# The row swap of two filter blocks moved from TensorE matmuls to GpSimd copies, and the order of the jobs set anew

## The chip, the cores and the metric

The kernel runs on one core of one Trainium2 chip. The metric is the device time of one execution in microseconds (us). The engines are named as in the profile: PE is TensorE's matmul, PEld its weight load, DVE is VectorE, ACT is ScalarE, POOL is GpSimd, SP is SyncE. A q behind a name (POOLq, SPq) is the engine's queue, which issues DMAs.

## The reference

Two independent branches, each 2048 tokens by 576 columns, and their results side by side. Everything is bfloat16.

```python
def _A_ref(x, wqkv, wo):            # H = 32 heads of 18; window W = 8, dilation 2
    q, k, v = ...                   # x @ wqkv, split by head
    idx = pos[:, None] - off[None, :]          # 8 earlier tokens, two apart
    logits = einsum(q, k[idx]) * scale         # -1e9 where idx < 0
    o = einsum(softmax(logits), v[idx])
    return o @ wo

def _B_ref(q, k, v, shift_k, ssm_k, ssm_D):
    k_shift = sum of 4 taps of k, weighted by shift_k
    kv = k_shift * v
    y = irfft(rfft(kv, 2S) * rfft(ssm_k, 2S))[:S]     # causal convolution per column
    y = y + kv * ssm_D
    return q * y

return concatenate([a, b], axis=-1)
```

## The kernel before, in words

Everything stays on chip. Branch A projects q, k and v transposed, multiplies q by shifted k on DVE (jobs `L`), sums over a head's 18 rows with matmuls (`G`), takes the softmax (`sm`), multiplies by v on DVE (`V`), sums over the window with identity matmuls (`A`) and projects (`O`). Branch B cuts the sequence into four blocks of 512 tokens. Each block of kv (`T` on DVE, then `M` on PE) and each block m of the filter `ssm_k` (`F`) is folded into even and odd parts, taken to the spectrum with sine tables (`x` for kv, `K` for the filter), multiplied block by block on DVE (`p`), summed on PE (`z`), and brought back (`i`, `b`, `g`).

The filter block m arrives by a transposing DMA in `kTok(m)`: partition = token within a chunk of 128, four chunks of 576 columns. `fold_filter(m)` (job `Fm`, L591 to L609) makes from chunks 0 to 3 the reversed sums with matmuls against 128x128 constants. A reversal by `flip1`/`flip2r` maps row p to row 128 - p, so that row 0 is left over: it has to come from row 0 of the other chunk. For blocks 0 and 1 the rows 0 of the chunks 0 and 1 are first swapped in memory, by six small DMAs of SP through a `spare` row (`first_rows`, job `Fr`, L577 to L581). For blocks 2 and 3 nothing is swapped: the reversal `flip0` leaves row 0 empty and an extra pair of matmuls against `corner` or `corner2`, which are zero but for one element, fills it in. `negate(m)` (job `Nm`, L589, on DVE) keeps a scaled copy of the old row 0. Behind the fold come two copies from PSUM on ACT (L604) and three accumulating DMAs that POOL issues (L606 to L609). The filter units `Kmcg` (L566, L567, copied out by ACT at L617) with c = 1 need the fold alone, those with c = 0 also the DMAs.

The order of the work is written by hand in the table `ORDER`: a list of job names. The program is recorded in that order, and each engine and each queue gets its instructions in it, one behind the other; an instruction waits for semaphores and holds up what stands behind it on its own engine. PSUM is four slots handed round in the order of the jobs. Other names in this document: `Lom` is a copy of a filter chunk by a DMA that POOL issues (L649), `SV` gives out the memory of v, `Z2` clears its pads on POOL (L366, L368), `RGn` regroups the weights of v on ACT (L779), `Un` are later accumulating DMAs of POOL (L625), `I` and `X5` are small preparations on PE.

## Time and profile before

| | |
|---|---|
| three runs | 207.15, 207.64, 208.27 us; median 207.64 |
| the profiled execution | 207.14 us, of which the span of the trace is 205.4 |
| PE busy | 197.5 us, 96% of the span |
| DVE busy | 187.9 us, 91% |
| ACT busy | 155.6 us, 76% |
| POOL busy | 64.0 us, 31% |
| DMA | 38.48 MB moved, mean 187 GB/s |

The share of busy time is an average over stages. PE and DVE are both nearly full; which of them ends a wait differs from stage to stage. In the rows below the first number of a timeline is the start in us from the span's start, the second the time; "x2" behind the shapes means two instructions merged into one row, with the time from the first start to the last end.

### The profile page before, as it was taken

Reading aid. Unit: us, or ns where it says so; the run is one execution under the profiler, and the core shown is the slowest. Engines: PE = TensorE matmul, PEld = TensorE weight load, DVE = VectorE, ACT = ScalarE, POOL = GpSimd, SP = SyncE. Lnnn points to the kernel's source line nnn. Section 1 sums busy time; section 2 is a strip of 40 time slices with the busy share of each in tenths; the row PEclk is TensorE's granted clock in tenths of the full one; section 3 lists DMA queues with packets and bytes.
Section 4 is the critical chain, followed back from the end, with each engine's and each line's share of the span. In section 5 each row is a group of like instructions: output and inputs, shape, how many; then the busy total and the mean of one; then the engine's idle time right before and its main releaser. Section 6 shows DMA issues by size and latency. Waiting matters only on the chain.

```text
span 205.4 us, 5096 instructions
## 1 busy us (share of the span) xinstructions
PE 197.5 (96%) x2112; PEld 111.2 (54%) x2122; DVE 187.9 (91%) x143; ACT 155.6 (76%) x223; POOL 64.0 (31%) x106
## 2 busy tenths in 40 slices
PE   7999999999999999999999999999999999999990
PEld 2534344434664656534354566766667767676560
DVE  7579999999999999999999999999999994599961
ACT  3798894858999999957776688876778877655660
POOL 8999910022266492300560000022090002030210
PEclk9999999999999999999999999999999999999997
DMA  6999999999239669999799990969899204853645
GB/s 201 304 321 250 213 317 351 187 220 297 84 48 125 91 91 193 176 200 219 153 246 203 245 224 14 177 229 264 163 246 246 91 3 165 180 153 122 173 158 150
DMA packets 34916, 38.48 MB, mean 187 GB/s; under 512 B 17523, under 2 KB 28911, under 8 KB 34894
## 3 DMA queue, kind: packets, MB, share of 16 engines
q1 hardware_dynamic: 26668, 24.29, 45.9%
q0 software_dynamic: 5760, 11.36, 29.3%
q10 hardware_dynamic: 2466, 2.51, 3.6%
q8 instruction: 16, 0.26, 0.5%
q14 instruction: 6, 0.05, 0.1%
HBM read 13.11 MB, written 4.72 MB: 87 GB/s over the span
## 4 chain that ended last, share of the span: by engine, by line
PE 67%; DVE 18%; DMA 7%; issue 4%; ACT 2%; SPq 1%; DVEq 0%
PE ps_z L968 10%; DVE tB L516 9%; PE ps_wo L887 8%; PE ps_inv L1003 7%; PE ps_acc L823 7%; PE ps_fx L681 7%; PE ps_proj L321 7%; DVE xw L519 7%; PE ps_fk L566 5%; PE ps_log L719 4%; DMA xw<-in_A_wqkv_dram 3%; DMA kj<-in_B_k_dram 2%; PE ps_fk L567 2%; DMA Ks<-in_B_ssm_D_dram 2%; PE ps_wo L879 2%
## 5 line engine op out<-in xcount | busy, mean ns | idle before, releaser
L321 PE MATMUL ps_proj<-xw 128*128 128x512 bf16 x151 | 37.3, 380 | 0.9 <-issue 0.6
L705 DVE TENSOR_TENSOR av<-qk 128x4096 bf16<-128x4096 bf16 (+1 forms) x16 | 31.7, 2013 | 0.1
L321 PEld LDWEIGHTS <-xw 128*128 128x128 bf16 x160 | 14.0, 98 | 18.2 <-issue 4.5
L981 ACT ACTIVATE av<-ps_z 128x768 bf16<-128x768 f32 x23 | 17.3, 810 | 6.5 <-PE ps_z L968 5.9
L617 ACT ACTIVATE Ks<-ps_fk 128x576 bf16<-128x576 f32 x32 | 19.4, 750 | 0.4 <-PE ps_fk L567 0.4
L516 DVE TENSOR_TENSOR tB<-kj,skb 128x4608 bf16<-128x4608 bf16 (+1 forms) x8 | 19.3, 2417 | 0.1
L354 ACT ACTIVATE qk<-ps_proj 128x1024 bf16<-128x1024 f32 x14 | 14.2, 1024 | 6.6 <-PE ps_proj L321 4.8
L683 ACT ACTIVATE xw<-ps_fx 128x576 bf16<-128x576 f32 x32 | 18.5, 666 | 0.7 <-PE ps_fx L681 0.7
L625 POOL DMA_DIRECT2D Ks<-Ks x8 | 11.0, 1654 | 26.0 <-PE ps_wo L879 18.6
L949 DVE TENSOR_TENSOR qk<-xw,Ks 128x2304 bf16<-128x2304 bf16 x14 | 18.6, 1353 | 0.0
L887 PE MATMUL ps_wo<-qk 128*128 128x288 bf16 x128 | 17.9, 287 | 0.0
L681 PE MATMUL ps_fx<-xw,TB 128*128 128x288 bf16 x128 | 17.5, 286 | 0.0
L566 PE MATMUL ps_fk<-Ks,TB 128*128 128x384 bf16 x62 | 16.3, 326 | 0.2
L1003 PE MATMUL ps_inv<-av,TI 128*128 128x288 bf16 (+1 forms) x112 | 15.9, 292 | 0.0
L823 PE MATMUL ps_acc<-av,ident 64*64 64x512 bf16 x160 | 15.3, 378 | 0.0
L567 PE MATMUL ps_fk<-Ks,TB 128*128 128x192 bf16 x62 | 15.2, 246 | 0.0
L681 PEld LDWEIGHTS <-TB 128*128 128x128 bf16 x128 | 12.0, 98 | 5.5 <-issue 2.1
L949 DVE TENSOR_TENSOR v<-xw,Ks 128x2304 bf16<-128x2304 bf16 x7 | 9.5, 1354 | 5.6 <-PE ps_z L968 5.6
L887 PEld LDWEIGHTS <-qk 128*128 128x128 bf16 x128 | 11.9, 98 | 4.8 <-issue 2.1
L812 DVE TENSOR_TENSOR av<-Ks,v 128x4096 bf16<-128x4096 bf16 x6 | 13.6, 2286 | 0.1
L354 ACT ACTIVATE v<-ps_proj 128x1024 bf16<-128x1024 f32 x9 | 9.3, 1035 | 5.8 <-PE ps_proj L332 3.0
L826 ACT ACTIVATE qk<-ps_acc 128x1024 bf16<-128x1024 f32 x8 | 8.2, 1023 | 7.1 <-PE ps_acc L823 7.1
(194 smaller groups left out, 447.1 us busy)
## 6 DMA issues: line engine op xcount, KB each, us to landing
Ks<-Ks POOLq DMA_DIRECT2D x8, 576.0 KB, 8.1
TB<-av SPq DMA_DIRECT2D x12, 256.0 KB, 5.3
kj<-in_B_k_dram SPq DMA_DIRECT2D x6, 504.0 KB, 7.0
vt<-in_B_v_dram SPq DMA_DIRECT2D x8, 288.0 KB, 5.1
Ks<-av SPq DMA_DIRECT2D x8, 256.0 KB, 5.8
out_dram<-qk ACTq DMA_DIRECT2D x5, 288.0 KB, 5.1
Ks<-in_A_x_dram SPq DMA_DIRECT2D x2, 576.0 KB, 5.1
xw<-in_A_wqkv_dram SPq DMA_DIRECT2D x2, 576.0 KB, 5.8
```

The lines of the kernel that those rows point to most:

```text
L321: nc.tensor.matmul(ps[:, jp, :], wq(kb, comp, 128 * ct, 128), xT(kb, 1024 * jj + 512 * jp, 512), **se)
L354: nc.scalar.activation(view(t, o + pad + 1024 * jj, [[512, 2], [1, 512]]), ps[:], ACT.Copy)
L516: tt(to, view(kj, row * D, [[D, n], [D, 4], [1, D]]), view(skb, row * D, [[D, n], [0, 4], [1, D]]), ALU.mult)
L566: nc.tensor.matmul(o[:, 0:2], w, rhs[:, 0:2], start=start, stop=stop)
L617: nc.scalar.activation(view(Ks, k_at(m, cs ^ (m & 1)) + 96 * gi, [[768, 3], [384, 2], [1, 96]]), acc3(ps), ACT.Copy, scale=(PSG, MSG)[cs][ ...
L681: nc.tensor.matmul(ps[:, pm, 0:HD], TX[:, 2 * pm + c, 128 * gi:128 * gi + 128], kv[:, 2 * c + pm, HD * h:HD * h + HD], start=(c == 0), sto ...
L705: tt(view(P, at, [[step, 4], [256, nj], [1, 256]]), view(t, o + 256 * hh, [[0, 4], [512, nj], [1, 256]]), view(tk, ok + 2 + 8 * ug + 256 * ...
L823: nc.tensor.matmul(acc[64 * o:64 * o + 64, h, :], ident[64 * h:64 * h + 64, 64 * h:64 * h + 64], view(P[s], 256 * u, [[2048, 2], [1, 256]] ...
L887: nc.tensor.matmul(ps[:, r, 0:HD], oT(hh, j + 2 * r, t)[:, o:o + 128], wo[:, t // 2, t % 2, HD * h:HD * h + HD], start=(t == 0 and not fli ...
L949: tt(product_home(n), view(xw, HB * XG[i] + QTR * t, [[HB, 3], [1, QTR]]), view(Ks, k_at(j - i, 0) + QTR * t, [[HB, 3], [1, QTR]]), ALU.mult)
L968: nc.tensor.matmul(view(ps, 512 * h, [[192, 2], [96, 2], [1, 96]])[o:o + 64], w[64 * h:64 * h + 64, 64 * h:64 * h + 64], pr[64 * h:64 * h ...
L1003: nc.tensor.matmul(ps[:, c, 0:n], TI[:, sl, pm, 128 * c:128 * c + 128], Yall(j % 2, pm, sl, slice(c0, c0 + n)), start=(pm == 0 and sl == 0 ...
```

## The change

Blocks 2 and 3 are now swapped too, by three copies each on POOL: old row 0 of chunk 0 to the spare row, row 0 of chunk 1 to chunk 0, spare to chunk 1 (`swap_rows`, jobs `RS3` and `RS2`). The fold then has the same form for all blocks: 8 matmuls and not 12. The constants `flip0`, `corner` and `corner2` go, and so do the POOL instructions that made them (a copy, two clears of 128x128 and two of one element); `pad` keeps their memory. `negate` of the blocks 2 and 3 reads the spare row and so comes behind the first copy. The table `ORDER` is written anew from its first line to its last.

```diff
-    flip0 = main.tile([128, 128], BF16, name="flip0")
-    corner = main.tile([128, 128], BF16, name="corner")
-    corner2 = main.tile([128, 128], BF16, name="corner2")
+    pad = main.tile([128, 384], BF16, name="pad")
...
-    nc.gpsimd.tensor_copy(flip0[:], flip1[:])
...
-    nc.gpsimd.memset(corner[:], 0.0)
-    nc.gpsimd.memset(corner2[:], 0.0)
-    nc.gpsimd.memset(corner2[0:1, 0:1], 2.0 ** 0.5)
-    nc.gpsimd.memset(corner[0:1, 0:1], 1.0)
...
-    spare = [view(Ks, k_at(1, 0) + D * m, [[1, D]])[0:1] for m in range(2)]
+    spare = [view(Ks, k_at(1, m // 2) + D * (m - m // 2), [[1, D]])[0:1] for m in range(NBL)]
+
+    def swap_rows(m):
+        for to, of in ((spare[m], row(m, 0)), (row(m, 0), row(m, 1)), (row(m, 1), spare[m])):
+            nc.gpsimd.tensor_copy(to, of)
...
     def negate(m):
-        nc.vector.tensor_scalar(minus_of(m), spare[m] if m < 2 else row(m, 0), -0.5 * ROOT, None, ALU.mult)
+        nc.vector.tensor_scalar(minus_of(m), spare[m], -0.5 * ROOT, None, ALU.mult)
...
     def fold_filter(m):
-        kt, swapped = kTok(m), m < 2
+        kt = kTok(m)
...
-            turns = [((flip2r, flip1)[c] if swapped else flip0, 1 - c), ((identn0, identn)[c], 2 + c)]
-            if not swapped:
-                turns.insert(1, ((corner2, corner)[c], c))
+            turns = [((flip2r, flip1)[c], 1 - c), ((identn0, identn)[c], 2 + c)]
...
         job(f"N{m}", negate, m)
+        if m > 1:
+            job(f"RS{m}", swap_rows, m)
```

Of the table, the lines around the two folds:

```diff
-    M00 k03b k12a M21 Lo0 q13b N1 k12b x020 x021 Z2 x001 RG2 k24a k24b L000 L002 x010 RG0 F3 F2 K312 L001 K311
-    K211 K212 RG1 K210 K310 RG3 G000 G001 L003 F1 N0 L004 G002 L010 G003 K300 G004 L012 K303 K313 K302 K201 K202
...
+    k12b k10a' N2 k10b q10b L000 M00 Z2 k24a' k24b L002 M21 k13a' k13b x020 x021 x001 x010 RG0 L001 RG1 RG2 F3
+    F2 G000 L003 K311 K313 K213 K312 K211 K310 G001 RG3 L004 G002 L010 K212 N1 F1 G003 L011 G004 L012 K302 K303
```

On POOL the place is the end of the filter's arrival. Before, behind the preparations (L501, L503), stand the copies Lo3, Lo2, Lo1 (L649), the accumulation of `ssm_D` (L578), Lo0, and then the clears of v's pads, the copy of a pad of q or k (L357) and the first DMA of the fold (L606):

```order
L501 MEMSET TB 1x512
L503 MEMSET TB 1x128 x4
L649 DMA Ks<-Ks 128x576 x3
L578 DMA Ks<-in_B_ssm_D_dram 1x16x36
L649 DMA xw<-Ks 128x576
L366 MEMSET v 128x4x16
L368 MEMSET v 64x16
L357 DMA qk<-qk 64x16
```

Now, with line numbers three to seven lower:

```order
L646 DMA Ks<-Ks 128x576 x3
L575 DMA Ks<-in_B_ssm_D_dram 1x16x36
L646 DMA xw<-Ks 128x576
L572 COPY Ks<-Ks 1x576 x6
L359 MEMSET v 128x4x16
L361 MEMSET v 64x16
L350 DMA qk<-qk 64x16
```

The six copies stand between Lo0 and the clears, and all of POOL's later work stands behind them.

On DVE the place is the change from the taps of the last kv block (the last of them L535) to the first products of branch A (L705). Before:

```order
L516 TENSOR_TENSOR tB<-kj,skb 128x4608
L519 TENSOR_TENSOR xw<-xw,tB 128x2304 x2
L535 TENSOR_TENSOR xw<-xw,vt 128x2304
L589 TENSOR_SCALAR Ks<-Ks 1x576 x3
L705 TENSOR_TENSOR av<-qk 128x4096
L705 TENSOR_TENSOR v<-qk 128x4x1024
```

Now:

```order
L509 TENSOR_TENSOR tB<-kj,skb 128x4608
L512 TENSOR_TENSOR xw<-xw,tB 128x2304 x2
L528 TENSOR_TENSOR xw<-xw,vt 128x2304
L586 TENSOR_SCALAR Ks<-Ks 1x576 x2
L702 TENSOR_TENSOR av<-qk 128x4096
L702 TENSOR_TENSOR v<-qk 128x4x1024
```

The first two negations, N3 and N2, stay ahead of the first product; N1 has moved behind it. Both wait for POOL now, N3 for the first copy and N2 for the fourth.

On ACT, around the copies of the folds F3 and F2 (L604, now L599), before:

```order
L683 ACTIVATE xw<-ps_fx 128x2x3x96 x3
L779 ACTIVATE xw<-Ks 128x576
L354 ACTIVATE qk<-ps_proj 128x1024
L683 ACTIVATE xw<-ps_fx 128x2x3x96
L779 ACTIVATE xw<-Ks 128x576
L604 ACTIVATE Ks<-ps_rev 128x576 x4
L617 ACTIVATE Ks<-ps_fk 128x6x96 x4
```

Now:

```order
L347 ACTIVATE qk<-ps_proj 128x1024
L680 ACTIVATE xw<-ps_fx 128x2x3x96 x4
L776 ACTIVATE xw<-Ks 128x576 x3
L599 ACTIVATE Ks<-ps_rev 128x576 x4
L612 ACTIVATE Ks<-ps_fk 128x6x96 x6
```

Three regroupings of v's weights, and not two, stand ahead of the folds' copies.

More of the change, by code (lines that the diff above doesn't have):

```diff
@@ L20 @@
 ORDER = """
-    I0 k02a I1 k00a k00b T0 T1 k01a' Lk2 S1 k02b k01b X5 q24a Lv2 T2 M01 Lk3 q24b Lv3 T3 Ex Lf3 q10a' q11a' N3
-    q11b q10b Lo3 k13a q12a' q12b k13b M10 Lf2 N2 Lo2 k10a Lf1 Lo1 k10b Lf0 M11 q13a' Lw Fr SV k11a' k11b k03a
-    M00 k03b k12a M21 Lo0 q13b N1 k12b x020 x021 Z2 x001 RG2 k24a k24b L000 L002 x010 RG0 F3 F2 K312 L001 K311
-    K211 K212 RG1 K210 K310 RG3 G000 G001 L003 F1 N0 L004 G002 L010 G003 K300 G004 L012 K303 K313 K302 K201 K202
-    K213 L011 F0 K203 G010 K200 K301 L013 U3 K103 G011 L014 G012 L100 RG4 K101 K100 G013 G014 K102 K111 K112
@@ L26 @@
-    K010 K110 K013 K113 U2 sm0a sm0b K012 K001 v24a v24b L101 G100 G101 sm0c K000 K011 L102 L103 v02a K002 K003
-    sm0d D0 G102 G103 v02b L104 G104 L110 L111 v00a' M20 v00b ak02 M30 D1 ak01 ak00 G110 L112 G111 L113 v01a'
-    v01b v11a v11b G112 L114 D2 M31 G113 V04 x030 G114 sm1a V11 v10a' v10b V10 x011 A04 v13a' sm1b v13b v03a
-    sm1c sm1d V12 v03b A10 v12a' x221 v12b x220 V13 V20 x330 A11 V21 x200 x211 x321 x031 V22 x300 A20 x301 x310
-    x000 x311 x331 Wl V23 x201 A21 D3 V34 A34 ax00 O000' D4 x231 x210 x230 x100 x131 x111 V40 V41 A40 O100' x101
@@ L31 @@
-    x110 x320 O001 V42 V43 A41 x130 U1 ak10 D5 V50 x120 Tx2 V51 x121 O010 p000 V52 A50 ax01 z000 O110 V53 ax02
-    p010 ax10 Tk2 O011' O101 A51 z010 O020' O021 p020 z020 Q0 p101 O111' i000 p200 i02880 p100 z100 z101 Q1 i001
-    i02881 p110 p111 z110 z111 p120 p121 z120 z121 p201 Tx3 z200 p202 z201 z202 i100 p210 z210 p211 b0288 p212
-    z211 z212 O120' i101 O121 b00 b10 O030' O031 i12880 p220 p221 z220 z221 p222 z222 Tk3 i200 p301 g0 p302
-    i12881 i201 O130 b1288 p300 z300 z301 z302 p303 z303 i22880 Q2 O131 p310 z310 p312 p311 p313 z311 z312 z313
@@ L36 @@
-    g1 Q3 i22881 i300 p320 p321 z320 p322 b2288 p323 i301 b20 g2 z321 z322 z323 b30 i3384L g30 g3384
+    T0 T1 k00a' k00b k02a Lk2 Lv2 Lk3 k02b S1 Ex k01a' k01b k03a Lv3 Lf3 k03b X5 k11a k11b q11a' Lo3 q11b Lf2
+    Lo2 Lf1 Lo1 M01 q24a Lf0 I1 q24b M10 Lw q12a' q12b T2 Fr I0 Lo0 q13a q13b k12a q10a T3 SV RS3 N3 RS2 M11
+    k12b k10a' N2 k10b q10b L000 M00 Z2 k24a' k24b L002 M21 k13a' k13b x020 x021 x001 x010 RG0 L001 RG1 RG2 F3
+    F2 G000 L003 K311 K313 K213 K312 K211 K310 G001 RG3 L004 G002 L010 K212 N1 F1 G003 L011 G004 L012 K302 K303
@@ new lines @@
+    K301 K200 K210 K203 N0 F0 K202 G010 K300 L013 K201 U3 RG4 G011 L014 G012 K103 K112 G013 K101 G014 K110 K102
+    L100 K113 K011 K100 K013 K111 sm0a sm0b K001 U2 v24a v24b G100 L101 G101 L102 sm0c sm0d K010 K000 K012 G102
+    L103 L104 K002 K003 D0 v02a v02b G103 L110 v00a G104 L111 x000 v00b G110 L112 ak02 v01a' v01b G111 L113
+    v11a' v11b G112 L114 M30 G113 x030 G114 D1 M20 v10a' v10b V04 v03a sm1a sm1b V10 v13a v13b A04 sm1c V11 D2
+    sm1d D3 V12 v03b A10 V13 D4 M31 v12a' v12b x321 x320 A11 x310 x011 V20 x201 x331 V21 x210 A20 V22 x200 V23
@@ new lines @@
+    V34 x330 x220 x301 x031 x211 A21 ax01 Wl A34 V41 O000' V40 U1 V42 x231 x221 D5 x230 Tx2 x130 x120 x311 A40
+    V43 x100 ax00 x121 x101 ak00 x300 O001 A41 O100' V50 x110 x131 x111 V51 A50 O010' O110 ak10 p000 V53 Tk2 V52
+    Q0 ak01 p010 z000 ax02 ax10 O011' O101 A51 p020 z010 p110 p101 O020' O021 z020 p100 Q1 O111' i000 i02880
+    p111 z100 p120 z101 p121 i001 p200 i02881 z110 p201 z111 z120 z121 z200 z201 Tx3 b0288 p202 z202 O120' p210
+    i100 p211 p212 z210 p222 z211 z212 Tk3 O030' p221 i101 O121 b00 p220 b10 O031' z220 p301 z221 z222 p303 g0
@@ L37 @@
+    Q2 i12880 i200 i12881 i201 p300 O130 z300 p302 z301 b1288 z302 z303 b20 i22880 O131 p310 p311 z310 p312 p313
+    g1 z311 z312 p322 z313 p320 p321 i22881 i300 z320 p323 b2288 i301 g2 z321 z322 z323 b30 i3384L Q3 g30 g3384
 """
```

## The prediction

> **What bounds the kernel now.** I read the page first: busy time and the chain that ended last.

> ```profile
> PE 197.5 (96%) x2112; PEld 111.2 (54%) x2122; DVE 187.9 (91%) x143; ACT 155.6 (76%) x223; POOL 64.0 (31%) x106
> ...
> PE 67%; DVE 18%; DMA 7%; issue 4%; ACT 2%; SPq 1%; DVEq 0%
> ```

> PE is full, two thirds of the chain are its own work, so a matmul less is worth its time, and a wait of PE is lost for good. The DVE share of the chain lies ahead of 50 us. Then I took the stage of the folds by windows of 5 us; each pair is busy time and count, PEclk the granted clock.

> ```profile
> core 0: us, PE busy (x) PEld busy (x) DVE busy (x) ACT busy (x) POOL busy (x), PEclk, DMA share, GB/s
> 50.00:55.00 5.00, 5.00 (x42) 2.80 (x42) 4.90 (x8) 4.95 (x7) 1.64 (x4) 1.00 0.53 172
> 55.00:60.00 5.00, 4.87 (x40) 3.55 (x39) 5.00 (x4) 5.00 (x9) 2.13 (x4) 1.00 0.02 3
> 60.00:65.00 5.00, 4.74 (x53) 2.31 (x52) 4.89 (x4) 5.00 (x8) 4.49 (x5) 1.00 1.02 143
> ```

> PE, DVE and ACT are all full here, POOL is not. Third, PE's own timeline through the folds F3 and F2 (54.67 to 57.63), the first filter unit, the first two head sums (61.06) and F1 (62.22):

> ```profile
> 54.67 0.41 PE L601 MATMUL ps_rev<-Ks,flip 128*128 128x288 bf16 x2
> 54.92 0.41 PE L601 MATMUL ps_rev<-Ks,corner 128*128 128x288 bf16 x2
> 55.16 0.41 PE L601 MATMUL ps_rev<-Ks,identn 128*128 128x288 bf16 x2
> ...
> 57.63 0.32 PE L566 MATMUL ps_fk<-Ks,TB 128*128 128x384 bf16 x1
> ...
> 58.42 0.32 PE L566 MATMUL ps_fk<-Ks,TB 128*128 128x384 bf16 x1
> ...
> 61.06 1.22 PE L719 MATMUL ps_log<-av,E 128*32 128x512 bf16 x16
> 62.22 0.42 PE L601 MATMUL ps_rev<-Ks,flip2r 128*128 128x288 bf16 x2
> ```

> Fourth, what POOL and DVE do when POOL has to read SBUF. The next two fences are timelines: the preparations early on, and the place where the copies are put in.

> ```profile
> 15.65 2.56 DVE L516 TENSOR_TENSOR tB<-kj,skb 128x4608 bf16<-128x4608 bf16 x1
> 15.82 2.53 POOL L287 COPY flip<-flip 128x128 bf16<-128x128 bf16 x1
> 18.24 2.75 DVE L519 TENSOR_TENSOR xw<-xw,tB 128x2304 bf16<-128x2304 bf16 x2
> 18.30 1.44 POOL L288 COPY flip2r<-flip 128x128 bf16<-128x128 bf16 x1
> 19.88 0.19 POOL L291 MEMSET corner<- 128x128 bf16 x1
> 21.02 1.36 DVE L535 TENSOR_TENSOR xw<-xw,vt 128x2304 bf16<-128x2304 bf16 x1
> 21.26 1.51 POOL L297 TENSOR_SCALAR ident<-ident 128x128 bf16<-128x128 bf16 x1
> 22.30 2.64 DVE L516 TENSOR_TENSOR tB<-kj,skb 128x4608 bf16<-128x4608 bf16 x1
> 22.74 2.59 POOL L298 TENSOR_SCALAR identn<-ident 128x128 bf16<-128x128 bf16 x1
> 25.40 0.51 POOL L501 MEMSET TB<- 1x512 bf16 x1
> ```

> ```profile
> 50.22 2.75 DVE L519 TENSOR_TENSOR xw<-xw,tB 128x2304 bf16<-128x2304 bf16 x2
> 50.44 0.86 POOL L578 DMA_DIRECT2D Ks<-in_B_ssm_D_dram  x1 [2.13 <-DVE tB L516]
> 51.00 0.88 POOL L649 DMA_DIRECT2D xw<-Ks  x1
> 53.01 1.36 DVE L535 TENSOR_TENSOR xw<-xw,vt 128x2304 bf16<-128x2304 bf16 x1
> 54.28 0.73 DVE L589 TENSOR_SCALAR Ks<-Ks 1x576 bf16<-1x576 bf16 x3
> 54.94 2.27 DVE L705 TENSOR_TENSOR av<-qk 128x4096 bf16<-128x4096 bf16 x1
> 57.14 2.27 DVE L705 TENSOR_TENSOR v<-qk 128x4096 bf16<-128x4096 bf16 x1
> ```

> A POOL copy that starts beside a DVE TENSOR_TENSOR lasts until that instruction's end and a little: L287 ends at 18.35, the DVE instruction at 18.21; L288 at 19.74, its neighbour (the first of two, 1.36 each) at 19.60. L297 and L298 do the same with 22.77 behind 22.38 and 25.33 behind 24.94. The MEMSET at 19.88, which reads nothing, takes 0.19 in the midst of a DVE instruction. So a POOL instruction with an input gets one chance per DVE instruction, at its end.

> [...]

> **The change part by part.**

> *Eight matmuls less.* Three pairs start 0.245 apart (54.67, 54.92, 55.16), 0.1225 a matmul: 8 x 0.1225 = 0.98 us off PE, in a stage where PE is full. The preparations that go (2.53, 0.19 and smaller) lie on POOL's early stretch, where nobody waits: nothing.

> *The price of a copy of 1x576.* No row shows one. From MEMSET: 128 columns take 0.19, 512 take 0.51, so 0.83 ns a column. The COPY of 128 columns lasts 0.14 beyond the DVE end, so one of 576 some 0.14 + 448 x 0.00083 = 0.51; I take 0.5 behind a DVE instruction and 0.6 alone. Low end 0.14, as the small copy; high end 1.75, if it went by L297's overhang of 0.39 x 4.5. I keep to the COPY, it is the same operation. DVE loses 0.08 to L297's 128 columns, so 0.08 x 4.5 = 0.36 to a copy (0 to 0.5).

> *When the swaps are done.* POOL is free of Lo0's issue at 51.00 + 0.88 = 51.88; what stands ahead of it in its queue, and SP's loads, are in the same order as before. DVE's second L519 runs until 52.97: copy 1 ends at 53.5. L535 is held to 53.36 and ends at 54.73; copy 2 ends at 55.2. N3 (0.25) goes in between or beside; copy 3 ends at 55.9, and with it RS3. Copy 4 ends at 56.5, N2 runs until 56.9, copy 5 slips in until 57.1, and the first product starts at 57.2 in place of 54.94. It runs 2.27, to 59.5: copy 6 starts beside it and ends at 60.0. So F3 can start at 56.0, F2 at 60.1.

> *PE at the folds.* The same jobs of PE stand ahead of F3 in both tables, so PE is there at 54.67 again: it waits 56.0 - 54.67 = 1.3 us. F3 takes 0.98, to 57.0; F2 waits 60.1 - 57.0 = 3.1. PE takes its queue in order, and the filter units that need F3 alone stand behind F2: nothing fills the wait.

> *What comes back.* ACT does all of RG0 to RG2 in the waits, ahead of the folds' copies, and so is ahead later, where PE waited for it: the unit at 57.63 took 0.79 and not 0.49, F1 until 63.72 and not 63.20.

> ```profile
> 63.72 0.61 PE L719 MATMUL ps_log<-v,E 128*32 128x512 bf16 x8
> ```

> That is 0.3 + 0.5 = 0.8 us to win back (0 to 0.8; I take all, since ACT gains more than that).

> *The granted clock.* Windows around the last matmuls:

> ```profile
> 1.30:4.72 3.42, 3.42 (x10) 1.27 (x10) 3.00 (x9) 1.87 (x3) 3.35 (x8) 1.00 0.80 255
> ...
> 195.86:199.28 3.42, 3.15 (x65) 2.31 (x54) 2.65 (x4) 1.85 (x4) 0.60 (x1) 1.00 0.25 83
> 199.28:202.69 3.41, 1.25 (x22) 0.74 (x19) 1.93 (x4) 0.68 (x2) 0.00 (x0) 1.00 0.93 263
> 202.69:205.40 2.71, 0.00 (x0) 0.00 (x0) 0.00 (x0) 0.00 (x0) 0.00 (x0) 0.50 0.23 57
> ```

> After a stretch of 3.41 us with 1.25 of PE work the clock is at 0.50. Between 54.67 and 60.1 PE would have 0.98 of work in 5.4 us. A stretch of 3.41 at half clock costs PE 1.7 of work; part of it lies in the wait itself: 0 to 1.7, I take 0.85.

> [...]

> *Work behind the copies.* POOL's clears of v's pads and F3's DMAs come at about 60.5 instead of 58.42 (the first POOL DMA of the fold). The units that need them stand behind F1 and four more head sums and are late by the same wait: nothing more, up to 0.5 if the cover is short. DVE is 2.3 behind at the first product and 0.36 more at copy 6; PE is behind by more, so DVE is not the bound.

> ```profile
> 58.42 1.28 POOL L606 DMA_DIRECT2D Ks<-Ks  x1 [2.26 <-ACT Ks L604]
> ```

> *The rest of the table.* The same work on each engine, elsewhere in the order. Ahead of the folds PE is full both ways; behind, single waits of some 0.3 us come and go: nothing, within 0.7 either way.

> The sum: -0.98 + 1.3 + 3.1 - 0.8 + 0.85 = +3.5 us on the profiled execution's 207.14: 210.6. The median before, 207.64, is 0.5 above that execution, so 210.6 is +1.4% by it.

> **The rivals.** (1) *In time, faster.* If a copy takes its low end of 0.14, copy 3 ends at 54.9 and F3 waits 0.3; copy 4 ends near 55.1, and copies 5 and 6 both begin before the first product does, some 0.25 us later: F2 doesn't wait. -0.98 + 0.3 = -0.7: 206.4. It is decided there: below 0.25 a copy, copy 6 is ahead of the product. For it: 0.14 is what the trace shows of a COPY. Against: that one has 128 columns, and MEMSET shows a price per column. (2) *No change.* The same short copies, but copy 6 falls beside the first product, from 55.4 to 57.7: F2 starts at 57.9, where PE came at 56.0: -0.98 + 0.3 + 1.9 - 0.8 = +0.4: 207.5. (3) *The clock stays*: the waits are 1.3 and 3.1, each shorter than the 3.41 of the rows' stretches, so every such stretch holds some work, if little: 3.5 - 0.85 = 2.65: 209.8. For it: only one stretch of the trace is so empty, and it is the last. [...] (4) *Copy 5 too is caught by the first product*: one more DVE instruction of 2.27 until F2: 212.9. What decides is whether POOL or DVE is first behind copy 4.

> **How the numbers follow.** Forecast 0.40, the clock stays 0.20, copy 5 caught 0.12, no change 0.14, in time 0.14. A measurement of this kernel tells about 0.5%, 1.0 us, from no change. Slower by more: 0.40 + 0.20 + 0.12 = 0.72; within: 0.14; faster by more: 0.14. The late cases alone span 209 to 213. Reaching to the case of no change and leaving out the one in time, the range is 206.9 to 213.0.

> **What the profile after would show.** Six COPY rows on POOL of 1x576, most ending just behind a DVE end; L000 near 57; a gap or a stretched wait of PE for POOL ahead of both folds, the second above 2 us; F2 near 60; the granted clock below 1.00 in a window behind. If the copies take 0.2 us each, or stand between DVE instructions without waiting, or F2 starts before 57.5, the forecast is wrong.

## The result, and the profile after

The changed kernel takes 217.01 us (median of 4 runs, 216.45 to 217.25), the kernel before 207.47 on the same chip (207.15 to 208.27): a ratio of 1.0436 with a 95% interval of 1.0412 to 1.0460. The direction was forecast. The size was not: 9.5 us, where 3.5 were forecast on the profiled execution and 3.0 on the median, and the time lies outside the range. The profiled execution of the changed kernel has a span of 215.1 us (before 205.4).

The page: busy time, the granted clock in 40 slices of 5.4 us, and the chain that ended last.

```profile
PE 199.4 (93%) x2114; PEld 112.1 (52%) x2114; DVE 189.6 (88%) x143; ACT 156.1 (73%) x223; POOL 71.9 (33%) x107
...
PEclk9999999999755999999999999999999999999998
...
PE 87%; POOL 6%; DMA 2%; ACT 1%; issue 1%; SPq 1%; DVE 0%; DVEq 0%; POOLq 0%
```

POOL wasn't in the chain before; now it has 6%, 13 us of 215, and the clock falls in three slices behind it (0.7, 0.5 and 0.5). PE's timeline through the two folds and the first head sum (G000, line 716):

```profile
53.81 0.29 PE L678 MATMUL ps_fx<-xw,TB 128*128 128x288 bf16 x1
56.23 0.41 PE L596 MATMUL ps_rev<-Ks,flip2r 128*128 128x288 bf16 x2 [2.14 <-POOL Ks L572]
...
65.02 0.64 PE L596 MATMUL ps_rev<-Ks,flip2r 128*128 128x288 bf16 x2 [7.11 <-POOL Ks L572]
...
67.03 1.04 PE L716 MATMUL ps_log<-av,E 128*32 128x512 bf16 x8
```

PE is free at 54.1, 0.6 sooner than before. F3 waits 2.14 us for the copies (line 572) and F2 7.11. G000 starts at 67.03; before it was at 61.06. The six copies as a group (shortest, median and longest in ns, first and last start) and the fifth of them alone, and then DVE's timeline in that stretch:

```profile
L572 POOL COPY Ks<-Ks x6: 657/772/7399, 52.8 to 64.3; 1x576 bf16<-1x576 bf16 x6
56.85 7.40 POOL L572 COPY Ks<-Ks 1x576 bf16<-1x576 bf16 x1
```

```profile
53.24 1.70 DVE L528 TENSOR_TENSOR xw<-xw,vt 128x2304 bf16<-128x2304 bf16 x1
54.87 0.76 DVE L586 TENSOR_SCALAR Ks<-Ks 1x576 bf16<-1x576 bf16 x1
56.83 0.30 DVE L586 TENSOR_SCALAR Ks<-Ks 1x576 bf16<-1x576 bf16 x1 [1.20 <-POOL Ks L572]
57.05 2.27 DVE L702 TENSOR_TENSOR av<-qk 128x4096 bf16<-128x4096 bf16 x1
59.25 2.27 DVE L702 TENSOR_TENSOR v<-qk 128x4096 bf16<-128x4096 bf16 x1
61.45 2.27 DVE L702 TENSOR_TENSOR av<-qk 128x4096 bf16<-128x4096 bf16 x1
68.18 2.29 DVE L702 TENSOR_TENSOR av<-qk 128x4096 bf16<-128x4096 bf16 x1 [4.46 <-ACT Ks L599]
```

A copy alone takes 0.657 us. Copies 1 and 2 end 0.52 behind the end of a DVE instruction, as forecast, and the next DVE instruction is stretched (L528 by 0.34, 1.70 and not 1.36; N3 by 0.47, 0.76 and not 0.29). I say of such a copy that it was let in at that end; one that is still running 0.6 us behind an end stayed out there. Copy 5 begins at 56.85, beside N2 (56.83), and ends at 64.25: it stays out at the end of N2, of the first product and of the second. These four instructions follow each other without a gap, each starting 0.07 before the end of the one ahead. 64.25 is 0.53 behind the third product's end, after which DVE has nothing to do.

The clock, in windows that follow its steps (columns as in the windows of the prediction):

```profile
53.27:56.68 3.41, 1.27 (x11) 0.88 (x10) 2.36 (x2) 3.41 (x6) 3.29 (x4) 1.00 0.17 49
56.68:60.10 3.42, 1.23 (x6) 0.62 (x5) 3.27 (x3) 3.20 (x4) 3.36 (x2) 0.50 0.04 8
60.10:63.50 3.40, 0.00 (x0) 0.00 (x0) 3.40 (x2) 0.00 (x0) 3.40 (x1) 0.50 0.01 0
63.50:66.92 3.42, 1.90 (x8) 1.02 (x7) 0.23 (x1) 0.21 (x1) 3.36 (x7) 0.50 0.01 1
66.92:70.34 3.42, 3.42 (x19) 1.59 (x19) 2.16 (x1) 1.82 (x4) 3.42 (x5) 0.50 0.89 121
70.34:73.75 3.41, 3.41 (x37) 2.01 (x36) 1.26 (x2) 3.40 (x6) 1.36 (x2) 1.00 0.98 131
```

Behind a window with 1.27 us of PE work the clock is at 0.50, and it stays there for 13.7 us, the last 3.4 of them with PE full.

### The profile page after: what moved, and what is told of

It reads as the page before. It is cut to its first block, busy times and chain, and to the rows that moved or that the text cites. A ratio compares the mean times of both kernels' runs of the same rounds, so it can differ in the third digit from the quotient of the medians.

```text
span 215.1 us, 5086 instructions
## 1 busy us (share of the span) xinstructions
PE 199.4 (93%) x2114; PEld 112.1 (52%) x2114; DVE 189.6 (88%) x143; ACT 156.1 (73%) x223; POOL 71.9 (33%) x107
## 3 DMA queue, kind: packets, MB, share of 16 engines
HBM read 13.11 MB, written 4.72 MB: 83 GB/s over the span
## 4 chain that ended last, share of the span: by engine, by line
PE 87%; POOL 6%; DMA 2%; ACT 1%; issue 1%; SPq 1%; DVE 0%; DVEq 0%; POOLq 0%
PE ps_proj L314 15%; PE ps_z L965 9%; PE ps_wo L884 8%; PE ps_inv L1000 7%; PE ps_acc L820 7%; PE ps_fx L678 7%; PE ps_fk L559 6%; POOL Ks L572 5%; PE ps_log L716 5%; PE ps_proj L431 3%; PE ps_fk L560 3%; PE ps_proj L325 2%; DMA Ks<-in_B_ssm_k_dram 2%; PE ps_rev L596 2%; PE ps_fold L537 2%; PE ps_proj L318 2%
## 5 line engine op out<-in xcount | busy, mean ns | idle before, releaser
L612 ACT ACTIVATE Ks<-ps_fk 128x576 bf16<-128x576 f32 x32 | 18.9, 683 | 1.9 <-PE ps_fk L560 1.8
L509 DVE TENSOR_TENSOR tB<-kj,skb 128x4608 bf16<-128x4608 bf16 (+1 forms) x8 | 19.3, 2417 | 0.1
L559 PE MATMUL ps_fk<-Ks,TB 128*128 128x384 bf16 x62 | 17.3, 343 | 0.0
L560 PE MATMUL ps_fk<-Ks,TB 128*128 128x192 bf16 x62 | 15.8, 255 | 0.0
L620 POOL DMA_DIRECT2D xw<-xw x2 | 2.5, 1251 | 31.8 <-ACT xw L680 31.8
```

Source lines behind the costliest of these rows:

```text
L509: tt(to, view(kj, row * D, [[D, n], [D, 4], [1, D]]), view(skb, row * D, [[D, n], [0, 4], [1, D]]), ALU.mult)
L559: nc.tensor.matmul(o[:, 0:2], w, rhs[:, 0:2], start=start, stop=stop)
L560: nc.tensor.matmul(o[:, 2], w, rhs[:, 2], start=start, stop=stop)
L612: nc.scalar.activation(view(Ks, k_at(m, cs ^ (m & 1)) + 96 * gi, [[768, 3], [384, 2], [1, 96]]), acc3(ps), ACT.Copy, scale=(PSG, MSG)[cs][ ...
```

## The experiments

Each ratio is to the kernel before, run beside it on the same chip (its medians there: 207.3 to 208.1 us).

### The table alone, and the swaps alone

The first takes the new table and the old folds (no `RS`, the corner matmuls back); the second the old table with the swaps at their place:

```diff
-    Lo0 q13b N1 k12b        (old table; N3 and N2 stood behind q11a' and Lf2)
+    Lo0 RS3 N3 RS2 N2 q13b N1 k12b
```

> The new order table with the old folds: no swaps, the eight corner matmuls back. Theory (the whole loss comes from the swaps, the table is worth nothing by itself): F3 starts near 54.1, where PE arrived in the changed kernel, F2 follows without a wait, the granted clock stays at 1.00 there, and the time is that of the kernel before, 207.5 within 1.0. Rival (the table itself is worse, and part of the 9.5 us is its): 209.5 or more.

> The old order table, the six copies at the same place of POOL's queue, behind Lo0. Theory (a copy gets in at the end of a DVE instruction only where the next DVE instruction waits for a semaphore; where it carries no wait, DVE runs on and the copy stays out): in this order the negate of block 1, with a wait for a DMA, follows the two negates, and the second product carries a wait for ACT. So copy 5 gets in near 57.3 and copy 6 behind the first product, near 60.2; F3 starts near 56.2, F2 near 60.3, no copy lasts over 3 us, and the time is 210 to 212. Rival (a copy waits until DVE has run out of work altogether): copy 5 lasts 7 us again, F2 starts at 65, 216 to 217.

Measured: the table alone 209.30 us, ratio 1.0056 (1.0034 to 1.0078); the swaps alone 217.69, ratio 1.0444 (1.0422 to 1.0467). The swaps make most of the loss: 4.4% in the old table, and 3.8% on top of the 0.56% of the new one. But my theory failed in both runs. The table is not free: some 1.2 us are its own. And in the old table copy 5 stayed out just as long, 7.6 us, though the DVE instructions behind N2 carry waits there. The copies of the swaps alone (shortest, median, longest); then, with the table alone, PE's waits in this stage (us in total, times, longest), and the windows on both sides of the clock's fall:

```profile
L572 POOL COPY Ks<-Ks x6: 657/762/7619, 53.4 to 65.1; 1x576 bf16<-1x576 bf16 x6
```

```profile
PE ps_log L719 <- ACT Ks L604: 2.4, 1, 2.4
```

```profile
57.18:60.59 3.41, 1.01 (x12) 0.50 (x12) 3.41 (x3) 3.41 (x6) 0.13 (x1) 1.00 0.02 1
60.59:64.00 3.41, 3.41 (x16) 2.13 (x14) 3.41 (x2) 2.55 (x6) 3.41 (x6) 0.50 0.57 84
```

In the new table G000 stands right behind F2, where six filter units stood in between: PE waits 2.4 us. The product had ended at 57.73; what ends the wait, at 59.67, is ACT's first copy of a fold (line 604), behind the three regroupings that now stand ahead of it. Here too the clock falls, behind a window with 1.01 us of work. Of this kernel's seven runs the fastest, 208.19, has a mean clock of 0.998, the other six 0.988 to 0.995.

### Copies 5 and 6 without products beside them, and products with gaps

```diff
-    ... spare[m], -0.5 * ROOT ...
+    ... spare[m] if m < 2 else row(m, 1), -0.5 * ROOT ...       (N waits for the last copy of its block)
```

```diff
+    def breath(hh, ug, ct):                  (jobs B0, B2: behind the first and the second product)
+        nc.vector.tensor_copy(pad[0:1, ct:ct + 1], <one element of that product>)
```

> The negates of blocks 2 and 3 read row 0 of the second half where it stands after the swap and not in the spare row (the same values), so DVE has to wait for the last copy of a block and no product can start before copy 6 is done. Theory (copy 5's 7.4 us are three DVE products that run without a wait between them): copies 5 and 6 take 0.66 each, done near 58.3, F2 starts there, the clock falls for one window or none, and the time is 208.5 to 211, though the products start 1.2 us later. Rival (the time was lost by something else in the table or behind the folds): 214 or more.

> The changed kernel with a DVE copy of one element behind the first and behind the second product, which reads that product's output and so waits for its end; two instructions more on DVE. Theory (the copy gets in where the next DVE instruction waits): copy 5 ends behind the first product, near 60.0 and lasts about 3 us, copy 6 ends behind the second, near 62.5, F2 starts near 62.6, and the time is 213 to 215.5. Rival (the copy waits until DVE runs out of products): copy 5 lasts 7 us or more again, F2 at 65 or later, 217 to 218.

Measured: 211.39 us, ratio 1.0158 (1.0102 to 1.0214), and 213.75, ratio 1.0283 (1.0212 to 1.0354); the first just above what was expected, the second as expected. The copies of the first, the copies of the second, and DVE of the second:

```profile
L572 POOL COPY Ks<-Ks x6: 657/657/1677, 52.8 to 57.7; 1x576 bf16<-1x576 bf16 x6
```

```profile
L572 POOL COPY Ks<-Ks x6: 657/1495/2998, 52.5 to 60.0; 1x576 bf16<-1x576 bf16 x6
```

```profile
57.15 2.27 DVE L702 TENSOR_TENSOR av<-qk 128x4096 bf16<-128x4096 bf16 x1
59.45 0.14 DVE L708 COPY pad<-av 1x1 bf16<-1x1 bf16 x1
59.52 2.57 DVE L702 TENSOR_TENSOR v<-qk 128x4096 bf16<-128x4096 bf16 x1
```

With no product beside them copies 5 and 6 take 0.66 each. With a gap behind the first product (57.15 + 2.27 = 59.42, the next instruction at 59.45) copy 5 is in there and lasts 3.0; the product behind it is stretched from 2.27 to 2.57. So the 7.4 us come of the three products that leave no gap, and two instructions more on DVE make the kernel 1.5% faster than the changed one (4.36 - 2.83). Of the 4.36% lost, 2.8 go when copies 5 and 6 meet no product (4.36 - 1.58).

### What lets a copy in where DVE leaves no gap

Copy 2 got in at the end of L528 although N3 stood ready (it starts at 54.87, L528 ends at 54.94). Why there, and not behind N2 or a product? Nine kernels asked, called e9 to e19 here. The second product ahead of the first, so that it carries a wait; a wait of the second product for an ACT instruction (`EW`), meant to be met before copy 5 begins or after; two fillers on DVE behind N2 or ahead of N3, with flat or nested operands; a long instruction in N2's place; and a POOL fill between copies 4 and 5:

```diff
-    k10a' N2 k10b q10b L000 M00 Z2 k24a' k24b L002
+    k10a' N2 L002 k10b q10b M00 Z2 k24a' k24b L000              (e9)
-    L002 ... RG0 L001 RG1 RG2
+    RG0 EW L002 L001 RG1 RG2                                    (e10; e11: RG0 RG1 EW L002 L001 RG2)
-    N2 k10b q10b L000
+    N2 k10b q10b Y0 Y1 L000                                     (e14 flat, e15 nested; e16: RS3 Y0 Y1 N3)
+    N2 behind L002; YL, 1x2304, waiting for copy 4, ahead of L000 (e17; e18 with a POOL fill of 1x128)
+    if m == 2 and to is spare[2]: nc.gpsimd.memset(pad[0:1, 0:384], 0.0)    (e19)
```

e9:

> The changed kernel with the second product ahead of the first (they have separate outputs): now the product in the second place carries a wait for ACT and DVE, the one in the third place carries none. Theory (a wait in the next instruction lets the copy in): copy 5 gets in behind the product in the first place, near 60, copy 6 then stays out through the second and third and ends near 64.4: the long copy is the sixth, and the time stays at 216 to 217.5. Rival 1 (one chance at each DVE end, whatever follows): copies end at 60.0 and 62.5, F2 at 62.6, 213 to 215.5. Rival 2 (a copy waits for DVE to run out of work): copy 5 lasts 7 us, copy 6 0.66.

e10:

> The changed kernel, with an ACT copy of one element into the place that the second product then overwrites, so that this product has to wait for ACT. Here that copy stands behind the first L776 of ACT, which ended at 56.4 in the changed kernel: the second product's wait is met before copy 5 begins (56.85). Theory (first come, first served: DVE's instructions whose waits are met stand in line ahead of a copy that comes later, and the copy gets in only behind them): nothing changes, copy 5 lasts 7.4 us, F2 starts near 65, 216.5 to 217.5. Rival (the copy is let in where the next DVE instruction is late enough to leave a gap): the same here.

e11:

> As the kernel before it in this list, with that ACT copy one place further back, behind the second L776 of ACT (57.6): the second product's wait is then met after copy 5 has begun and 1.5 us before the first product ends, so DVE has no gap. Theory (first come, first served): copy 5 is let in at the first product's end and lasts about 3.0 us; copy 6 then finds the second and third product ahead of it and lasts about 4.5, F2 starts near 64.7, 216 to 217.5. Rival (only a gap on DVE lets a copy in): copy 5 lasts 7.4 us and copy 6 0.66.

e14:

> The changed kernel with two multiplications more on DVE between N2 and the first product, 128x1152 with operands that lie in one piece, no wait between them (they work on the dead table tB). One question: what decides at a DVE end without a gap. Theory A (the pattern of the operands: the products read in three nested strides, and only between such instructions does DVE keep its turn): copy 5 gets in at the end of the first filler, 0.5 us behind it. Theory B (DVE keeps its turn whenever the next instruction is ready, and the two cases of L528 have another reason): copy 5 stays out until DVE has a gap.

e15:

> The same two fillers with operands in three nested strides, as the products read theirs. Theory A: copy 5 stays out between the fillers. Theory B: it stays out as well. Only if copy 5 got in at the flat fillers and stays out here is the pattern the reason.

e16:

> The two flat fillers between L528 and N3, where copy 2 got in at the end of L528 although the next DVE instruction, N3, was there without a gap. N3 carries a wait for POOL, the filler carries none. Theory A (pattern): copy 2 gets in at the end of L528 as before. Theory C (the next instruction's own wait, even one already met, lets the copy in, if it is for something other than ACT): copy 2 stays out at L528, and at the first filler, and gets in at the second filler's end, ahead of N3.

e17:

> The changed kernel with one DVE instruction more, a multiplication of 1x2304 into the dead table tB that waits for copy 4 as N2 did; N2 itself stands behind the second product. Copy 5 then arrives at the start of a DVE instruction that lasts 0.6 us or more, where it arrived 0.27 us ahead of N2's end before. Theory E (a copy gets in at the end of the DVE instruction in whose course it arrives, unless it arrives only 0.1 to 0.3 us ahead of that end; one that has missed that end stays out until DVE has a gap): copy 5 ends 0.5 behind the added instruction, copy 6 arrives in the course of the first product and ends 0.5 behind it, near 61; F2 starts there, and the time is 212 to 214, with more work on DVE than in the changed kernel. Rival (DVE keeps its turn while its next instruction is ready, whenever the copy came): copy 5 lasts 8 us or more, 217 to 219.

e18:

> The kernel with the long DVE instruction in N2's place, and a POOL fill of 1x128 (0.2 us, it reads nothing) between copies 4 and 5: copy 5 then begins 0.2 us behind that DVE instruction's start and 0.5 ahead of its end, and no longer 0.03 behind its start. Theory N (a copy that begins within 0.03 us of a DVE instruction's start, as every copy that stayed out did, loses its place until DVE has a gap; one that begins well inside a DVE instruction gets in at its end): copy 5 ends 0.5 behind the long instruction, copy 6 behind the first product, F2 near 61, 212 to 214. Rival: copy 5 stays out again, about 8 us, 217 to 219.

e19:

> The changed kernel with nothing but a POOL fill of 1x384 (some 0.4 us) between copies 4 and 5: copy 5 begins 0.2 to 0.3 us behind the first product's start, well inside it. Theory N: copy 5 gets in at the first product's end, 59.85, copy 6 behind the second, 62.6, F2 starts there and the time is 213 to 215, though POOL does more. Rival (DVE keeps its turn from instruction to instruction whenever the copy came): copy 5 ends at 64.25 as in the changed kernel, 216.5 to 217.5.

Measured, in this order: 216.32 us, 216.61, 216.90, 218.55 (one run), 218.76 (one run), 217.56 (one run), 217.71, 217.26, 216.75; ratios of the timed ones 1.040 to 1.048. Wherever a theory would have let copy 5 in, it stayed out, except in e16, where the fillers ahead of N3 let copies 3 and 4 in and copy 5 found N3 ending. The copies of e9, e11, e14, e16 and e18, a fence for each:

```profile
L572 POOL COPY Ks<-Ks x6: 657/1027/7402, 52.5 to 64.5; 1x576 bf16<-1x576 bf16 x6
```

```profile
L572 POOL COPY Ks<-Ks x6: 657/912/7401, 52.7 to 64.5; 1x576 bf16<-1x576 bf16 x6
```

```profile
L572 POOL COPY Ks<-Ks x6: 657/1137/8737, 52.1 to 65.7; 1x576 bf16<-1x576 bf16 x6
```

```profile
L572 POOL COPY Ks<-Ks x6: 657/1190/7227, 52.8 to 58.7; 1x576 bf16<-1x576 bf16 x6
```

```profile
L572 POOL COPY Ks<-Ks x6: 653/1202/8028, 52.2 to 65.2; 1x576 bf16<-1x576 bf16 x6
```

In each of them one copy, the fifth (in e16 the sixth), waits out all of DVE's run, and ends 0.52 to 0.53 behind it. Out as the reason are a wait that the next product carries (e9 to e11; in e10 as in e11 it was met behind copy 5's start, `EW` ending at 57.45 and 57.51 and copy 5 starting at 56.69 and 56.99, so the early case was not made), and the length of the instruction in whose course the copy comes (e17: 0.75 us). The pattern of the operands is out as well: the same flat fillers let a copy in at their ends ahead of N3 (e16) and keep it out behind N2 (e14). DVE in these two kernels, e16 first:

```profile
55.09 2.34 DVE L707 TENSOR_TENSOR tB<-tB 128x1152 bf16<-128x1152 bf16 x2
57.36 1.48 DVE L586 TENSOR_SCALAR Ks<-Ks 1x576 bf16<-1x576 bf16 x2
```

```profile
57.09 1.41 DVE L707 TENSOR_TENSOR tB<-tB 128x1152 bf16<-128x1152 bf16 x2
```

1.41 for two undisturbed fillers, 2.34 for two with a copy let in ahead of each. The last two kernels are weaker evidence: in e18 copy 5 began only 0.06 behind the start of the long instruction (0.2 was meant), in e19 0.14 ahead of the first product's start and not within it. But another kernel, the one with early swaps in the new table (below), has a copy that begins 0.03 behind the start of an undisturbed L528 and is let in at its end, where L509 follows without a gap and is stretched from 2.56 to 3.02 (POOL's row between DVE's two):

```profile
42.65 1.36 DVE L528 TENSOR_TENSOR xw<-xw,vt 128x2304 bf16<-128x2304 bf16 x1
42.67 1.85 POOL L572 COPY Ks<-Ks 1x576 bf16<-1x576 bf16 x1
43.92 3.02 DVE L509 TENSOR_TENSOR tB<-kj,skb 128x4608 bf16<-128x4608 bf16 x1
```

So coming just behind a start is not the reason either. It is shown that a gap on DVE let a waiting copy in: copy 1 of the changed kernel at a gap of 0.03 us (L512 ends at 53.21, L528 starts at 53.24), copies 5 and 6 of the kernel with gaps at 0.03 and 0.04. Three products without one kept copy 5 out for 7.4 us. What decides at an end without a gap stays open: in the kernels with swaps, all ends that let a copy in stand ahead of DVE's last wait for a copy (N2, or the long instruction in its place), all that kept one out are that instruction's own and later ones, and no run shows why. A second difference goes with it and was not tested by itself: every copy that stayed out had begun while a TENSOR_SCALAR ran (N2 or the long instruction; in the changed kernel at 56.85, N2 running from 56.83 to 57.13), and those let in at an end without a gap had begun while a TENSOR_TENSOR ran (L528 or a filler), but for copy 5 of e16, 0.10 ahead of N3's end. No copy of these runs begins within a product.

### The half clock

Matmuls of no use ahead of F3 (9) and of F2 (31), so that PE isn't idle in the two waits:

```diff
+            nc.tensor.matmul(ps[:, 0, :], ident[:], view(TB, XO, [[1, 512]]), start=True, stop=True)
```

> The changed kernel with matmuls of no use (128x512, their results are not read) in PE's two waits: 9 ahead of F3, 31 ahead of F2. Theory (2.7 to 3.1 us of the loss are the half clock from 56.7 to 70.3, since PE had little work in the windows ahead): the granted clock stays at 1.00, F2 still starts near 65.0 and PE does the work behind it at full clock: 213.8 to 214.8. Rival (the half clock is covered by ACT or DVE and costs nothing): 216.5 to 217.5.

Measured: 216.56 us (214.74 to 217.63), ratio 1.0400 (1.0322 to 1.0478): by the time, the rival. The trace tells more. The clock stays at 1.00 behind both waits (1.00 in each window of 5 us from 50 to 75); the same DVE instructions late in the kernel, in the changed kernel and then with the added matmuls:

```profile
161.68 1.35 DVE L946 TENSOR_TENSOR qk<-xw,Ks 128x2304 bf16<-128x2304 bf16 x1
...
165.49 2.62 DVE L946 TENSOR_TENSOR qk<-xw,Ks 128x2304 bf16<-128x2304 bf16 x2
```

```profile
158.98 1.35 DVE L954 TENSOR_TENSOR qk<-xw,Ks 128x2304 bf16<-128x2304 bf16 x1
...
165.20 2.63 DVE L954 TENSOR_TENSOR qk<-xw,Ks 128x2304 bf16<-128x2304 bf16 x2 [2.33 <-DMA out_dram<-qk]
```

At 161 us this kernel is 2.70 us ahead, and had been since 73 us; 0.24 of that it had at F2 already (64.78 and not 65.02). Then a store out of qk, whose place the next product needs, takes 2.33 of it back. So the half clock cost some 2.5 us where it arose, and this profiled run gave most of that back at another wait 90 us later. The fastest of the four runs, 214.74, may have kept it; it has no trace.

### Copies far ahead of the folds, and no copies at all

Both tables with the swaps right behind the loads of their halves (`Lo3 RS3`, `Lo2 RS2`; in the old table N3 and N2 follow at once, in the new one they stay where they were); the kernel before without the corner matmuls, which leaves out what they add to row 0; and three small DMAs for a block in place of the copies:

```diff
-            if not swapped:
-                turns.insert(1, ((corner2, corner)[c], c))
```

```diff
+    def swap_out(m):    nc.gpsimd.dma_start(<two spare rows>, <rows 0 of chunks 0 and 1>)      (ROm)
+    def swap_in(m):     nc.gpsimd.dma_start(row(m, 0), aside[m]); nc.gpsimd.dma_start(row(m, 1), spare[m])   (RIm)
+    Lo3 RO3 k13a ... RI3 N3 Lo2 RO2 k10a Lf1 Lo1 RI2 N2 k10b
```

> The new table with the copies and negates of blocks 3 and 2 right behind the loads of their halves, ten microseconds and more ahead of the folds. Theory (what hurts is the place, not the copies): the copies end before 53 however long they wait there, neither fold waits, the clock stays at 1.00, and PE keeps its eight matmuls less: 206.2 to 207.2, about 1 us below before. Rival (the copies take DVE's time wherever they stand, 0.36 to 0.5 us each, and DVE sets the end of that early stretch): 2 to 3 us more, 208.5 to 210.

> The old table, with the same early place for copies and negates (blocks 3 and 2, each behind the load of its half). Theory: as with the new table, no wait at the folds and eight matmuls less, 206.2 to 207.2. Rival (copies cost DVE time on the early chain): 208.5 to 210.

> The kernel before, old table, with the eight corner matmuls left out and nothing in their place; it leaves out the part of row 0 of blocks 2 and 3 that they add. It shows what the change could bring at most in the old table. Theory (a matmul less is worth its time, PE being full): 0.5% less, 207.1 to 207.3 against 208.1, or by that ratio against the runs of before of this call. Rival (DVE sets the first head sums, PE would only wait there): no change, within 0.2%.

> The old table, no corner matmuls, and the rows of blocks 2 and 3 swapped by three small DMAs of POOL's queue for each block (both rows out to the spare place, then each back crosswise), ten microseconds ahead of the folds; no POOL copy. Theory (the copies' harm is DVE's time and their waits for DVE; DMAs have neither): the folds start without a wait, DVE is not late, and the time is that of the kernel with nothing in place of the corner matmuls, 0.3 to 0.5% below before. Rival (small DMAs behind the large loads land too late or hold POOL's later DMAs up): PE waits ahead of F3 or F2, 0.5% or more above before.

Measured: early in the new table 209.85 us, ratio 1.0080 (1.0066 to 1.0094); early in the old table 209.45, ratio 1.0069 (1.0052 to 1.0085); no corner matmuls 207.60, ratio 0.9998 (0.9984 to 1.0013); by DMA 210.96, ratio 1.0135 (1.0098 to 1.0172). The rival was right on the time in all four, but not always for its reason. In the new table the 0.80% is hardly more than what the table costs alone (0.56%, with intervals that overlap), and PE's longest wait is again one for ACT's first copy of a fold, 3.0 us. So it is the old table that shows what early copies cost.

The copies in the old table, then DVE under them (undisturbed, L528 and L512 take 1.36 and L509 2.56, as L535, L519 and L516 did before), then PE's longest wait:

```profile
L572 POOL COPY Ks<-Ks x6: 693/1674/2876, 42.5 to 52.6; 1x576 bf16<-1x576 bf16 x6
```

```profile
42.67 1.70 DVE L528 TENSOR_TENSOR xw<-xw,vt 128x2304 bf16<-128x2304 bf16 x1
44.30 3.01 DVE L509 TENSOR_TENSOR tB<-kj,skb 128x4608 bf16<-128x4608 bf16 x1
47.34 1.70 DVE L512 TENSOR_TENSOR xw<-tB 128x2304 bf16<-128x2304 bf16 x1
...
57.41 2.27 DVE L702 TENSOR_TENSOR av<-qk 128x4096 bf16<-128x4096 bf16 x1
```

```profile
PE ps_log L716 <- DVE av L702: 1.5, 1, 1.5
```

Every copy takes 0.34 to 0.45 us from DVE, which leads the work there: the first product starts at 57.41 and not 54.94, and PE waits for it behind the folds.

The kernel without corner matmuls is the one that counts most. Eight matmuls less, nothing in their place, and no time gained. PE there:

```profile
54.72 0.41 PE L599 MATMUL ps_rev<-Ks,flip 128*128 128x288 bf16 x2
...
56.44 0.41 PE L599 MATMUL ps_rev<-Ks,identn 128*128 128x288 bf16 x2
57.66 0.32 PE L566 MATMUL ps_fk<-Ks,TB 128*128 128x384 bf16 x1 [0.81 <-ACT Ks L602]
```

The folds end a microsecond earlier, and the first filter unit starts at 57.66, before at 57.63: it waits for ACT's copies of F3. DVE, which runs without a wait here, starts its products at the times of before to within 0.25 us. What the change was to bring isn't there to be had in this order of the work.

By DMA, PE waits 2.7 us for the first product, because DVE waits for a DMA ahead of it; PE's wait, and DVE's:

```profile
PE ps_log L722 <- DVE av L708: 2.7, 1, 2.7
```

```profile
58.01 0.41 DVE L591 TENSOR_SCALAR Ks<-Ks 1x576 bf16<-1x576 bf16 x1 [2.37 <-DMA Ks<-Ks]
```

This is N1, which writes where the swap of block 2 keeps a row, and the last DMA of that swap was issued only at 56.36, not ten microseconds ahead of the folds. The rival had seen the late landing, but PE's wait ahead of F3 or F2 and not of the first product. A better place for that row was not tried, since nothing is to be gained over 0.9998.

## Why the prediction was right or wrong

*What bounds the kernel.* "PE is full, two thirds of the chain are its own work, so a matmul less is worth its time": wrong. PE, DVE and ACT were all near 100% in the windows I quoted, and I let the chain's share over the whole span decide for this stage. The -0.98 us is 0 (0.9998, measured in the old table).

*When the swaps are done.* This is the step that failed. Copies 1 to 4 went as worked out (56.79 for copy 4, forecast 56.5), and the price of a copy was right: 0.657 alone (forecast 0.6), 0.52 behind a DVE end (0.5), 0.34 to 0.47 off DVE (0.36). "Copy 5 slips in until 57.1" and "one chance per DVE instruction, at its end" did not hold: copy 5 ended at 64.25, and F2 could start at 65.0 and not at 60.1. Rival 4 saw copy 5 caught, but for one DVE instruction more, 2.27; it was three, and copy 5 was let in neither at the end of N2 (57.13) nor at those of two products (59.32 and 61.52). My four early rows stood at DVE ends with a gap of 0.03 us behind them, or, for L297, at the end of L535 (now L528) at 22.38, where L516 had started at 22.30 and L297 was let in all the same, ending at 22.77. They were no evidence for products in a row, which POOL had never met in the trace.

*PE at the folds.* 2.14 for 1.3 at F3, since PE came 0.6 earlier and copy 3 was 0.3 later; 7.11 for 3.1 at F2, by the step above. These two waits are why the direction was right.

*What comes back* (-0.8): not separated by any run. In the changed kernel PE's only waits between 45 and 120 us are the two for the copies, so the 0.26 within F1 is gone; of the rest nothing is known.

*The granted clock.* 0.85 within 0 to 1.7 was forecast, for one window at half; it was four, and some 2.5 us on the way to 161 us. The cause was right: the windows with 1.27 us of PE work here and 1.01 with the table alone each have the half clock behind them. Neither was empty, so that some work in a window keeps the clock, as rival 3 had it, did not hold. Counted in steps of 3.41 us (the half clock from 56.68 to 70.34 is four of them), the fullest window of these traces at full clock with the half clock behind it (with the long instruction, e17) and the emptiest with the full clock behind it (the products with gaps) are:

```profile
53.92:57.33 3.41, 1.43 (x12) 1.02 (x11) 2.21 (x3) 3.41 (x6) 3.28 (x4) 1.00 0.14 41
52.38:55.80 3.42, 1.50 (x13) 1.06 (x11) 3.30 (x3) 3.42 (x6) 3.30 (x4) 1.00 0.39 119
```

*The rest of the table*, "nothing, within 0.7": 0.56%, 1.2 us. I looked at which filter units stood behind F2 only to say that they could not fill the wait, and not at G000, which now stood ahead of them and waits 2.4 us for ACT with the table alone.

*Work behind the copies* (nothing to 0.5): not separated by any run; the clears and the fold's DMAs came at 64.9 and later, with F2 itself.

The sum as the runs have it, in per cent of the kernel before: table 0.56, swaps on top of it 3.8 (4.36 - 0.56), of which 2.8 go when copies 5 and 6 meet no product. Each of these ratios is known to 0.2 to 0.6 either way.

## What to carry to other kernels

Where three engines are full in the same stage, take the work away with nothing in its place before paying for its removal: here that showed that eight matmuls were worth nothing (0.9998). A GpSimd copy of 1x576 beside VectorE cost VectorE 0.34 to 0.47 us here, and one waited 7.4 us for a whole run of VectorE instructions that follow without a gap, not for one; put such a copy where VectorE idles, or make VectorE wait for it (0.66 each here). In a hand-set order, look at what stands directly behind the moved work on the waiting engine, and count the granted clock behind each wait (0.50 for 13.7 us here).
